# Five exponent buffers, another order at the handover, and other engines for the early block's split

## The chip, the cores and the metric

One NeuronCore of a Trainium2 chip runs the whole program. The metric is the device time of one execution in microseconds, the median of several runs.

## The reference, cut to what matters

The program is an attention with capped scores, followed by a mixture of experts in which every token goes to one expert of eight. All numbers are 32-bit floats.

```python
# q, k, v: 8 batches, 12 heads, 448 positions, 64 wide
scores = q @ k.T / sqrt(64)
scores = cap * tanh(scores / cap)
attn = exp(scores - max); attn /= attn.sum(-1) + 1e-9
x = (attn @ v) as 3584 tokens of 768
# w_gate 768x8, w1 8x768x1024, w2 8x1024x768
e = argmax(x @ w_gate); g = softmax(x @ w_gate)[e]
out = g * (max(x @ w1[e], 0) @ w2[e])
```

## The kernel before, in words

**Attention.** The work is 24 quads, each four heads of one batch, and a quad has seven tiles of 64 keys, so there are 168 tiles in 84 steps of two tiles. In step k the program issues, for tiles 2k and 2k+1, the score products on TensorE (`scores`, tile `sp`, two PSUM buffers) and the tanh on ScalarE (`tanh`, from `sp` into half of a buffer `pt`). Then come the exponential of the step before on ScalarE (`expo(k-1)`, in place in `pt`) and, on TensorE, the products with the values for tiles 2k-6 and 2k-5 (`pv`, `values`, accumulated in `po`). VectorE then adds up exponentials (`adds(k-2)`, tiles `acc` and `p4`). One `pt` buffer holds a step, so `tanh` of step k can only start when `values` and `adds` have read step k-4: four buffers. The two `po` banks hold one quad. The first value product of a new quad is therefore held back by a step (`held`), until VectorE has copied the old quad out (`outp`, tile `ot`).

Between the steps run the routing of finished batches (`sums`, `logits`, `rec_p` on TensorE; `rec_v`, `log_v`, `route_v`, `place_v`, `turn` on VectorE), written into a table by step with `at` and carried out with `do`. Each engine takes its instructions in the order in which they are written. [...]

**The early block.** While batches 4 to 8 are still in attention, 448 tokens of the first three batches are collected for the first expert block, called -2. From step 66 on, each of its six column blocks k is scaled (`scale_x`), transposed (`trans_x`, tile `xt`, two buffers) and split into a high part `xh` and the remainder `xl` (`split_x`, before: both on GpSimd). These six pieces come three steps apart.

**The handover.** After the last step the two `sp` buffers become four other PSUM banks (`ps_h`, `ps_z`). TensorE then computes the remaining value products, with the first products of block -2 in between: `up_mm(-2, 0)` is 18 matmuls over `xh`, `xl` and the weights' high and low parts. The rest of the mixture of experts follows, eight more blocks after block -2, with `up_mm`, `up_ev` and `down` in turn, weights and tokens gathered by indirect DMA from GpSimd's queue. `RING` is the space, in bytes of each SBUF partition, for the descriptors of GpSimd's DMAs.

Of the kernel before, what the change touches and what calls it, by code (L numbers as in the profile page):

```python
# [4 lines left out]
F32 = mybir.dt.float32  # L5
# [5 lines left out]
ALU = mybir.AluOpType  # L11
# [4 lines left out]
B, H, S, D = 8, 12, 448, 64  # L16
# [7 lines left out]
QB = S // 32  # L24


RING = 4096
QN = 11
QR = QB - QN

# [96 lines left out]
def attention_moe(tc, qT, kT, vL, capd, wgL, w1a, w1b, w2a, w2b, cst, cmk, out):  # L127
    nc = tc.nc
    V, A, G, PE = nc.vector, nc.scalar, nc.gpsimd, nc.tensor
# [10 lines left out]
    op = pools("op")  # L140
    pb = pools("pb")
# [13 lines left out]
    m = {"xp": xp}  # L155
# [89 lines left out]
    pts = {}  # L245
# [14 lines left out]

    def tanh(t):
        if t % 2 == 0:
            pts[t // 2] = pb.tile([128, 2, 2, S], F32, name="pt", bufs=4)
        scale = qsc if t < KT else 1.0
        A.activation(out=pts[t // 2][:, t % 2], in_=sps.pop(t)[:, :, 0:S], func=AF.Tanh, scale=scale)  # L265

# [4 lines left out]
    def expo(k):  # L271
        A.activation(out=pts[k], in_=pts[k], func=AF.Exp, scale=capt)  # L272
# [464 lines left out]
    def width(j):  # L737
        return LARGE if large(j) else SMALL

    def groups(j):  # L740

        return QB if large(j) else 8
# [53 lines left out]
    def chunk(pool, name, at=(0, 0)):  # L796
        return [
            pool.tile([128, DM + 8], F32R, name=name + i)[:, o : o + DM] for i, o in zip("hl", at)
        ]
# [4 lines left out]
    def high(i, f, e=A):  # L804
        w, r = ((w1s, w1r), (w2s, w2r))[i - 1]
        (e.copy if e is A else e.tensor_copy)(out=w[f][0], in_=r[f // 4][:, f % 4, :])
# [88 lines left out]
    xts = {}  # L895

    def trans_x(j, k, g=None):
# [2 lines left out]
        xt = xts[j, k] = m["xp"].tile([128, LARGE], F32, name="xt", bufs=XT)[:, 0:n]  # L900
        V.transpose(out=xt.rearrange("p (q j) -> p q j", j=32), in_=xg[:, g, 32 * k : 32 * k + 32])  # L901

    def split_x(j, k, e, eh=A, g=None):
        g = g or slice(0, groups(j))
        c = slice(32 * g.start, 32 * g.stop)
        xt = xts.pop((j, k))
        xh = m["xh"][:, k, c]
        (eh.copy if eh is A else eh.tensor_copy)(out=xh, in_=xt)  # L908
        e.tensor_tensor(out=m["xl"][:, k, c], in0=xt, in1=xh, op=ALU.subtract)
# [19 lines left out]
    def up_mm(j, f, r=None):  # L929
        r = r or slice(0, width(j))  # L930
        xh, xl = m["xh"], m["xl"]
        wh, wl = w1s[f]
        if (j, f) not in phs:
            phs[j, f] = m["ps_h"].tile([128, 512], F32, name="ph")[:, 0 : width(j)]
        ph = phs[j, f][:, r]
        i = 0
        for k in range(KC):
            c = slice(128 * k, 128 * k + 128)
            for w, x in ((wh, xh), (wh, xl), (wl, xh)):
                PE.matmul(ph, w[:, c], x[:, k, r], start=i == 0, stop=i == 3 * KC - 1)  # L940
                i += 1
# [101 lines left out]
    def at(step, when, f, *a):  # L1043
        tasks.setdefault((step, when), []).append((f, a))
# [37 lines left out]
    n_first = (KT * B_FIRST * NQ - 1) // 2 + 11  # L1082
# [11 lines left out]
    for i in range(QB):  # L1094
        at(n_first + 8 + i, "v", load_x, -2, range(i, i + 1))
    for k in range(KC):
        t = n_first + 24 + 3 * k
        at(t, "v", scale_x, -2, range(k, k + 1))
        at(t + 1, "v", trans_x, -2, k)
        at(t + 2, "v", split_x, -2, k, G, G)  # L1100
    w1s[0] = chunk(xp, "w10")
    at(n_first + 20, "v", split_w1, 0, G, G)

# [11 lines left out]
    def values(k):  # L1115
        nonlocal held
        last = None
        ready = held + [2 * k - 6, 2 * k - 5]
        held = [ready.pop()] if ready[-2] % KT == KT - 1 else []
        for t in ready:  # L1120
            pv(t)
            if t % KT == KT - 1:
                last = t // KT
        return last
# [29 lines left out]
    m["ps_h"] = pools("ps_h", bufs=2, space=PSUM, side="right", **tw)  # L1154
    m["ps_z"] = pools("ps_z", space=PSUM, side="right", **tw)
    expo(STEPS - 1)
    assert values(STEPS) is None
    up_mm(-2, 0)
    high(1, 2)
    low(1, 2, G)  # L1160
    adds(STEPS - 2)
# [289 lines left out]
```

## Time and profile before

| | us |
|---|---|
| median of 3 runs | 805.44 (804.15 to 806.04) |
| profiled execution | 804.61 |
| its span, first to last instruction | 802.7 |
| attention steps, ScalarE's first tanh to its last exponential | 6.7 to 304.2 |
| block -2 and the eight others | 306.9 to the end |

The page gives busy shares over the whole span: TensorE 97%, VectorE 69%, ScalarE 56%, GpSimd 51%. They are means over stages with different limits, so each stage is read by itself. PE is TensorE's matmuls, PEld its weight loads, DVE is VectorE, ACT is ScalarE, POOL is GpSimd. "Idle before" is the time for which an engine had nothing to do before an instruction, with the instruction that ended it.

### The profile page before, as it was taken

The numbers are of one execution on the slowest core, as the hardware profiler recorded it, in microseconds if no ns is written. First come the engines' busy times: TensorE is split into PE (matmuls) and PEld (weight loads), VectorE is DVE, ScalarE is ACT, GpSimd is POOL, SyncE is SP. The second block draws the span as 40 slices with busy tenths as digits, with TensorE's granted clock in tenths as the row PEclk, the third lists the DMA queues.
The fourth block names the chain that finished last, engine by engine and source line by source line (L and its number), as shares of the span: only waits on it lengthen the run. The fifth ranks groups of instructions, "written<-read, shape, count | busy, mean of one in ns | idle before, by whom it ended". The sixth has DMA issues, their size and how long they took to land.

```text
span 802.7 us, 15069 instructions
## 1 busy us (share of the span) xinstructions
PE 780.4 (97%) x5984; PEld 571.4 (71%) x5984; DVE 551.7 (69%) x908; ACT 449.4 (56%) x534; POOL 411.4 (51%) x400
## 2 busy tenths in 40 slices
PE   8999999999999989999999999999999999999995
PEld 3343434343434436899999999999999999999995
DVE  2788897998899997878549448358347357357730
ACT  7999999999998992343334324224224233234520
POOL 1001330318474465353785784884884884764742
PEclk9999999999999999999999999999999999999998
DMA  8325573488879602493441133542510252454211
GB/s 283 102 107 162 118 210 129 116 228 208 236 171 254 187 17 58 81 345 112 165 172 41 51 109 140 212 135 109 218 50 31 67 183 98 173 190 165 71 57 52
DMA packets 37102, 112.62 MB, mean 140 GB/s; under 512 B 8609, under 2 KB 15699, under 8 KB 34464
## 3 DMA queue, kind: packets, MB, share of 16 engines
q0 software_dynamic: 18528, 63.93, 25.5%
q1 hardware_dynamic: 18208, 47.43, 19.0%
q8 instruction: 49, 0.80, 0.4%
q10 hardware_dynamic: 288, 0.23, 0.1%
q14 instruction: 29, 0.24, 0.1%
HBM read 101.69 MB, written 22.85 MB: 155 GB/s over the span
## 4 chain that ended last, share of the span: by engine, by line
PE 81%; ACT 7%; DVE 6%; issue 2%; POOL 2%; DMA 1%; POOLq 0%; DVEq 0%; ACTq 0%
PE ph L940 29%; PE y L975 22%; PE po L322 10%; PE sp L255 10%; PE y L983 4%; ACT pt L265 4%; ACT pt L272 3%; PE ms L349 2%; DVE acc L277 2%; POOL xg L745 1%; PE po L975 1%; PE z L975 1%; PE ms L975 1%; DMA xg<-xd,xi 1%; DVE ot L329 1%
## 5 line engine op out<-in xcount | busy, mean ns | idle before, releaser
L952 ACT ACTIVATE hb<-ph 128x448 fp32r<-128x448 f32 (+1 forms) x69 | 35.0, 508 | 264.1 <-PE ph L940 263.4
L745 POOL DMA_INDIRECT xg<-xd,xi x114 | 139.7, 1225 | 36.4 <-issue 27.0
L953 DVE SCALAR_TENSOR_TENSOR hb<-ph,hb 128x448 fp32r<-128x448 f32 (+1 forms) x69 | 39.5, 572 | 168.7 <-ACT hb L952 168.7
L255 PE MATMUL sp<-qk 64*64 64x448 f32 x1344 | 147.5, 549 | 5.3 <-ACT pt L265 5.2
L272 ACT ACTIVATE pt<-pt,capt 128x1792 f32<-128x1792 f32 x84 | 152.4, 1816 | 0.0
L265 ACT ACTIVATE pt<-sp 128x896 f32<-128x896 f32 x161 | 140.0, 934 | 16.4 <-DVE acc L277 6.8
L322 PE MATMUL po<-pt,vr 64*64 64x448 f32 x1344 | 144.5, 541 | 4.4 <-DVE ot L329 4.4
L755 POOL DMA_INDIRECT out<-ys,xi x98 | 104.4, 1066 | 27.3 <-issue 27.3
L322 PEld LDWEIGHTS po<-pt,vr 64*64 64x64 f32 x1344 | 54.0, 134 | 79.2 <-issue 69.0
L255 PEld LDWEIGHTS sp<-qk 64*64 64x64 f32 x1344 | 43.9, 132 | 82.0 <-ACT pt L265 57.3
L277 DVE TENSOR_TENSOR acc<-acc,pt 128x1792 f32<-128x1792 f32 (+1 forms) x36 | 61.5, 1707 | 4.1 <-ACT pt L272 4.1
L485 POOL DMA_DIRECT2D xd<-w2r x12 | 8.4, 710 | 104.8 <-DVE mx L456 104.6
L940 PE MATMUL ph<-xh,qk 128*128 128x448 f32 (+2 forms) x228 | 60.5, 340 | 0.0
L277 DVE TENSOR_TENSOR acc<-pt 128x896 f32<-128x896 f32 (+1 forms) x36 | 51.4, 1428 | 11.0 <-ACT pt L272 10.7
L516 POOL DMA_INDIRECT ids<-tokg,slots x32 | 43.5, 1360 | 25.6 <-DVE slots L510 16.5
L908 ACT CAST xh<-xt 128x448 fp32r<-128x448 f32 (+2 forms) x54 | 25.8, 490 | 33.5 <-DVE xt L901 33.5
L745 POOL DMA_INDIRECT w1r<-in_w1b,widx x7 | 10.5, 1495 | 66.4 <-DVE w17l L811 66.4
L940 PEld LDWEIGHTS ph<-xh,qk 128*128 128x128 f32 x228 | 40.8, 188 | 3.4 <-issue 0.7
L940 PE MATMUL ph<-xl,qk 128*128 128x448 f32 (+2 forms) x114 | 38.6, 339 | 0.0
L329 DVE COPY ot<-po 128x448 f32<-128x448 f32 x48 | 27.5, 614 | 15.5 <-PE po L322 15.4
L901 DVE STREAM_TRANSPOSE xt<-xg 128x448 f32<-128x448 f32 (+2 forms) x60 | 32.4, 549 | 1.4
L890 DVE TENSOR_TENSOR xg<-xg,sc 128x448 f32<-128x448 f32 (+2 forms) x60 | 30.2, 551 | 0.3
(368 smaller groups left out, 1789.9 us busy)
## 6 DMA issues: line engine op xcount, KB each, us to landing
vr<-in_vL SPq DMA_DIRECT2D x24, 448.0 KB, 4.9
qk<-in_qT SPq DMA_DIRECT2D x23, 448.0 KB, 5.9
qk<-in_kT SPq DMA_DIRECT2D x22, 448.0 KB, 5.8
xd<-yt POOLq DMA_DIRECT2D x16, 346.5 KB, 6.3
xd<-w2r POOLq DMA_DIRECT2D x12, 346.5 KB
w1r<-in_w1a SPq DMA_DIRECT2D x8, 384.0 KB, 7.1
w1r<-in_w1b SPq DMA_DIRECT2D x8, 384.0 KB, 8.0
w2r<-in_w2b SPq DMA_DIRECT2D x8, 384.0 KB, 8.8
```

The source lines that it names most:

```text
L255: PE.matmul(sp[w, r, 0:S], kr[h, c, 64 * g : 64 * g + 64], qr[h, c, :], start=True, stop=True)
L265: A.activation(out=pts[t // 2][:, t % 2], in_=sps.pop(t)[:, :, 0:S], func=AF.Tanh, scale=scale)
L272: A.activation(out=pts[k], in_=pts[k], func=AF.Exp, scale=capt)
L277: V.tensor_tensor(out=o, in0=a, in1=b, op=ALU.add)
L322: PE.matmul(pvs[m][c][w, 0:S], vr[r, g, j, :], pt[r, j, :], start=g == 0, stop=g == KT - 1)
L329: V.tensor_copy(out=ot, in_=pvs[m][c][:, 0:S])
L516: i = G.indirect_dma_start(out=ids, out_offset=bass.IndirectOffsetOnAxis(ap=slots[0:p, c : c + 1].bitcast(U32), axis=0), in_=tokg[0:p, c, ...
L745: G.indirect_dma_start(out=dst, out_offset=None, in_=src, in_offset=bass.IndirectOffsetOnAxis(ap=idx.bitcast(U32), axis=0), bounds_check=b ...
L755: i = G.indirect_dma_start(out=dst, out_offset=bass.IndirectOffsetOnAxis(ap=idx.bitcast(U32), axis=0), in_=src, in_offset=None, bounds_che ...
L940: PE.matmul(ph, w[:, c], x[:, k, r], start=i == 0, stop=i == 3 * KC - 1)
L953: V.scalar_tensor_tensor(out=hl, in0=ph, scalar=0.0, in1=hh, op0=ALU.max, op1=ALU.subtract)
L975: PE.matmul(y[k][:, 0:LARGE], w[:, c], h, start=f == 0 and i == 0, stop=f == FC - 1 and i == 2)
```

## The change

- `pt` has five buffers and not four.
- `RING` is 2048 bytes and not 4096.
- Of the early block, the high part is copied by ScalarE, between the two tanhs and the exponential of a step, and the low part is computed by VectorE at the end of that step. This is one step later than GpSimd's turn was. The sixth piece is scaled and transposed one step earlier.
- At the handover `up_mm(-2, 0)` is written before `values(STEPS)` and not after it.

```diff
-RING = 4096
+RING = 2048
...
-            pts[t // 2] = pb.tile([128, 2, 2, S], F32, name="pt", bufs=4)
+            pts[t // 2] = pb.tile([128, 2, 2, S], F32, name="pt", bufs=5)
...
+    def high_x(j, k):
+        A.copy(out=m["xh"][:, k], in_=xts[j, k])
+
+    def low_x(j, k):
+        V.tensor_tensor(out=m["xl"][:, k], in0=xts.pop((j, k)), in1=m["xh"][:, k], op=ALU.subtract)
...
-        t = n_first + 24 + 3 * k
+        t = n_first + 24 + 3 * k - k // 5
         at(t, "v", scale_x, -2, range(k, k + 1))
         at(t + 1, "v", trans_x, -2, k)
-        at(t + 2, "v", split_x, -2, k, G, G)
+        at(t + 3, "act", high_x, -2, k)
+        at(t + 3, "v", low_x, -2, k)
...
-    assert values(STEPS) is None
     up_mm(-2, 0)
+    assert values(STEPS) is None
```

TensorE at the handover, before (`sp` are the last scores, `po` value products, `ph` the products of block -2):

```order
L255 MATMUL sp<-qk 64x448 x8
L322 MATMUL po<-pt,vr 64x448 x16
L940 MATMUL ph<-xh,w10h 128x448
L940 MATMUL ph<-xl,w10h 128x448
L940 MATMUL ph<-xh,w10l 128x448
```

and now, with the 18 matmuls into `ph` shortened to their first three and last one:

```order
L255 MATMUL sp<-qk 64x448 x8
L322 MATMUL po<-pt,vr 64x448 x4
L946 MATMUL ph<-xh,w10h 128x448
L946 MATMUL ph<-xl,w10h 128x448
L946 MATMUL ph<-xh,w10l 128x448
...
L946 MATMUL ph<-xh,w10l 128x448
L322 MATMUL po<-pt,vr 64x448 x28
L946 MATMUL ph<-xh,qk 128x448
```

Only the last tile of the old quad (4 rows of `po`; the trace counts each as two) stays ahead of the block's products. The seven tiles of the last quad follow them in one piece.

VectorE in the last step, before (`ot` is the copy of the old quad out of PSUM, `xt` the sixth transposed piece):

```order
L901 STREAM_TRANSPOSE xt<-xg 128x448
L329 COPY ot<-po 128x448 x2
L277 TENSOR_TENSOR acc<-pt 128x896
L503 TENSOR_TENSOR pos<-ms,base 128x32
L505 TENSOR_TENSOR base<-base,ms 128x8
L507 TENSOR_TENSOR pos<-pos,ob 128x32
L510 TENSOR_REDUCE slots<-pos 128x4
L277 TENSOR_TENSOR acc<-pt 128x896
```

and now:

```order
L329 COPY ot<-po 128x448 x2
L277 TENSOR_TENSOR acc<-pt 128x896
L503 TENSOR_TENSOR pos<-ms,base 128x32
L505 TENSOR_TENSOR base<-base,ms 128x8
L507 TENSOR_TENSOR pos<-pos,ob 128x32
L510 TENSOR_REDUCE slots<-pos 128x4
L907 TENSOR_TENSOR xl<-xt,xh 128x448
L277 TENSOR_TENSOR acc<-pt 128x896
```

The sixth low part now stands on VectorE behind the copies, one addition and four small instructions. Its transpose stands a step ahead of where it was.

ScalarE over the last three steps, now (`xh` the fifth and the sixth high part, which before were not on this engine):

```order
L265 ACTIVATE pt<-sp 128x896 x2
L904 CAST xh<-xt 128x448
L272 ACTIVATE pt<-pt,capt 128x1792
L265 ACTIVATE pt<-sp 128x896 x2
L471 ACTIVATE ex<-df 128x32
L272 ACTIVATE pt<-pt,capt 128x1792
L265 ACTIVATE pt<-sp 128x896 x2
L904 CAST xh<-xt 128x448
L272 ACTIVATE pt<-pt,capt 128x1792 x2
L806 CAST qk<-w1r_117 128x768
```

An exponential waits behind each of the six casts.

## Rows read from the trace of the kernel before

**Rows 1.** The page, first section: busy time, share, instructions of each engine.
```profile
PE 780.4 (97%) x5984; PEld 571.4 (71%) x5984; DVE 551.7 (69%) x908; ACT 449.4 (56%) x534; POOL 411.4 (51%) x400
```

**Rows 2.** Busy time by stretch: length, PE, PEld, DVE, ACT, POOL, TensorE's clock, DMA.
```profile
240.00:303.00 63.00, 57.26 (x684) 25.18 (x678) 61.44 (x90) 56.92 (x54) 31.37 (x24) 0.99 0.56 156
...
304.00:306.00 2.00, 2.00 (x16) 1.21 (x12) 1.97 (x4) 0.91 (x2) 1.06 (x2) 0.57 0.00 0
```

**Rows 3.** ScalarE's waits from 26 to 240 us: us in total, times, longest.
```profile
ACT pt L265 <- DVE acc L277: 4.1, 3, 1.4
ACT pt L265 <- PE po L322: 4.1, 9, 0.7
```

**Rows 4.** Timeline of ScalarE: start, us, instruction, idle before it.
```profile
102.96 1.73 ACT L265 ACTIVATE pt<-sp 128x896 f32<-128x896 f32 x2 [0.72 <-PE po L322]
...
141.67 1.73 ACT L265 ACTIVATE pt<-sp 128x896 f32<-128x896 f32 x2 [1.35 <-DVE acc L277]
```

**Rows 5.** The chain that ended last, in order of time: start, us, work.
```profile
120.50 1.79 PE sp L255 x16
...
128.30 1.50 PE sp L255 x16
129.81 1.50 PE po L322 x16
```

**Rows 6.** Timeline of TensorE, one wait for ScalarE.
```profile
149.34 1.79 PE L255 MATMUL sp<-qk 64*64 64x448 f32 x16 [0.69 <-ACT pt L265]
```

**Rows 7.** Groups by shape, whole span: the same split on ScalarE and VectorE.
```profile
L908 ACT CAST xh<-xt 128x448 fp32r<-128x448 f32 x30 | 16.5, 568 | 16.5 <-DVE xt L901 16.5
...
L909 DVE TENSOR_TENSOR xl<-xt,xh 128x448 fp32r<-128x448 f32 x30 | 17.9, 596 | 0.6
```

**Rows 8.** Groups of VectorE by shape, 240 to 303 us: count, busy us, mean ns.
```profile
L277 DVE TENSOR_TENSOR p<-acc 128x896 f32<-128x896 f32 x5 | 6.0, 1208 | 0.1
...
L890 DVE TENSOR_TENSOR xg<-xg,sc 128x448 f32<-128x448 f32 x6 | 4.9, 809 | 0.0
...
L269 DVE TENSOR_SCALAR qk<-qk,qsc 128x896 f32<-128x896 f32 x4 | 3.9, 980 | 0.0
...
L478 DVE TENSOR_SCALAR gt<-gt 128x4 f32<-128x4 f32 x2 | 1.1, 540 | 0.1
```

**Rows 9.** Three of these groups from 100 to 220 us.
```profile
L277 DVE TENSOR_TENSOR p<-acc 128x896 f32<-128x896 f32 x9 | 9.7, 1073 | 0.2
...
L269 DVE TENSOR_SCALAR qk<-qk,qsc 128x896 f32<-128x896 f32 x10 | 6.8, 680 | 0.0
...
L478 DVE TENSOR_SCALAR gt<-gt 128x4 f32<-128x4 f32 x3 | 0.5, 179 | 0.1
```

**Rows 10.** Tile xg, 380 to 440 us: duration in ns, least, median, most.
```profile
L890 DVE TENSOR_TENSOR xg<-xg,sc x6: 619/620/626, 421.0 to 423.7; 128x448 f32<-128x448 f32 x6
```

**Rows 11.** Timelines of VectorE and of GpSimd at the same time.
```profile
297.17 1.78 DVE L890 TENSOR_TENSOR xg<-xg,sc 128x448 f32<-128x448 f32 x1
...
296.65 1.82 POOL L811 TENSOR_TENSOR qk<-w1r,qk 128x768 fp32r<-128x768 f32 x1
```

**Rows 12.** Timelines at the handover: TensorE, then ScalarE, then VectorE.
```profile
298.48 0.93 PE L322 MATMUL po<-pt,vr 64*64 64x448 f32 x8
302.76 4.19 PE L322 MATMUL po<-pt,vr 64*64 64x448 f32 x24 [3.34 <-DVE ot L329]
...
310.73 3.24 PE L322 MATMUL po<-pt,vr 64*64 64x448 f32 x32
...
300.69 3.50 ACT L272 ACTIVATE pt<-pt,capt 128x1792 f32<-128x1792 f32 x2
...
302.12 1.12 DVE L329 COPY ot<-po 128x448 f32<-128x448 f32 x2
```

**Rows 13.** Timelines of GpSimd and VectorE: gathers for the second block.
```profile
366.34 1.02 POOL L745 DMA_INDIRECT xg<-xd,xi  x1 [0.30 <-issue]
...
370.43 0.20 DVE L881 TENSOR_TENSOR sc<-xg,idt 128x42 f32<-128x42 f32 x1 [0.33 <-DMA xg<-xd,xi]
```

More of the change, by code (lines that the diff above doesn't have):

```diff
@@ L1156, in attention_moe @@
     expo(STEPS - 1)
+    up_mm(-2, 0)
     assert values(STEPS) is None
-    up_mm(-2, 0)
     high(1, 2)
```

## The prediction

> **What bounds the kernel now.** I read the page first: TensorE is busy for 97% of the span [rows 1]. A time can therefore only fall where TensorE waits or runs below its pace, and I looked for those places stage by stage. After the handover there are next to none, so whatever is won before about 314 us should move the rest of the program forward as a whole. In attention, the stretch from 240 to 303 us is the odd one [rows 2]: VectorE is busy for 61.4 of 63 us there, while TensorE is idle for 5.7 and ScalarE for 6.1. VectorE sets the pace in it, because the early block's scaling and transposing comes on top of its additions. Earlier, from 26 to 240 us, TensorE and ScalarE are nearly balanced, and ScalarE's waits name a missing `pt` buffer: 4.1 us for VectorE's additions, 4.1 us for a held-back value product [rows 3].
>
> **Five buffers, 26 to 240 us.** A wait of ScalarE is only worth what TensorE loses by it. Two kinds repeat, in a pattern of two batches (about 74 us).
> The first is the wait of 0.72 us for a value product [rows 4]. In the steps that follow, ScalarE sets the pace: the two score products then take 1.79 us in the chain, against 1.50 when nothing holds them, and the value products take 1.50 [rows 5]. So a step is 3.29 us there and 3.0 at TensorE's own pace. Four such steps offer 4 x 0.29 = 1.2 us, so an earlier ScalarE passes its whole 0.7 us on. It occurs twice before 240 us: 1.4 us. The other short waits of that kind fall where TensorE is working off the sums and has no gap, and I count them as nothing.
> The second is the wait of 1.35 us for an addition [rows 4]. Some eight microseconds later TensorE stands still for 0.69 us and its next score product is stretched by 0.29 us [rows 6]: 0.98 us lost of 1.35. It occurs three times: 2.9 us.
> Sum: 4.3 us. The ends: three times the bare 0.69, or 2.1 us, and all of ScalarE's waits for a buffer, 4.1 + 4.1 = 8.2 us [rows 3].
>
> **The split, 240 to 303 us.** GpSimd loses six copies and six subtractions; ScalarE gains six copies of 0.57 us and VectorE six subtractions of 0.60 us, as in the same shapes of later blocks [rows 7].
> ScalarE: five copies lie before the last step, 5 x 0.57 = 2.8 us, beside 6.1 us of idle time, most of which the fifth buffer frees. They cost nothing as long as VectorE is the later one. If that cover goes, they cost 2.8 us. An exponential is queued behind each, and value products and additions wait for it. A copy would wait if its `xt` were late; that transpose is issued two steps ahead.
> VectorE: five subtractions before the last copies, 5 x 0.60 = +3.0 us. Against this stands something that the list of removed instructions hides: VectorE is slowed by GpSimd. The same instructions take longer from 240 to 303 us than from 100 to 220 us [rows 8, 9]: the fold 1.21 against 1.07 us (five: 0.7), the scaling of q 0.98 against 0.68 (four: 1.2), the small scalar operation 0.54 against 0.18 (two: 0.7); and the scaling of the gathered rows takes 0.81 against 0.62 us [rows 8, 10] (six: 1.1). That is 3.7 us. One row of it stays: 1.78 us for a scaling at 297.17, under the subtraction of a weight split on GpSimd that the change leaves where it is [rows 11], 1.16 us above the usual. So 2.6 us go and 3.0 come: VectorE is 0.4 us later at the last copies. Ends: 3.0 us later if the slowing only moves, 0.7 us earlier if the weight split's share goes as well.
> The Trainium skill ("SBUF — State Buffer", section "Who interferes with whom") says that a VectorE instruction with two SBUF inputs and a GpSimd one that reads SBUF exclude each other for the whole of the one that started first. The pair at 297 us agrees [rows 11]. It also speaks against the change: the new subtraction has two SBUF inputs, so the weight split's last subtraction on GpSimd can hold it up; the price of that is worked out below from those rows.
>
> **The handover.** Before [rows 12]: the last value product of the old quad ends at 298.48 + 0.93 = 299.4. TensorE then waits until VectorE has copied the old quad out (302.12). The next 24 matmuls take 4.19 us, though 16 take 1.50 [rows 5], so 24 should take 2.25: the clock is at 0.57 of full speed after the wait, its lower level of 1.2 GHz [rows 2]. Then 18 matmuls of the block until 310.73 (3.8 us), and 32 more until 313.97. The work is 2.25 + 3.8 + 3.0 = 9.05 us in 14.55: 5.5 us are lost.
> After: the block's 18 matmuls need a PSUM bank from the last tanhs, which end before the exponential at 300.69, so they start by 300.8. The first 16 need nothing late and end near 304.2. The last two need the sixth `xl`. VectorE: copies at 302.12 + 0.4 = 302.5 until 303.6, one addition (1.07, as the fold of the same size [rows 9]) until 304.7, four small instructions of 0.18 [rows 9] until 305.4, the subtraction until 306.0. So TensorE waits about 1.8 us, ends the block's products at 306.4 and then runs 56 matmuls of value products in 5.25 us, until 311.65. The exponentials have been ready since 304.2. Against 313.97 that is 2.3 us won. What is late next is that subtraction. At the old VectorE pace minus 0.7 us it would be 3.4 us won; at plus 3.0 us it would be -0.3.
>
> **Ring.** Halving `RING` costs nothing if GpSimd never fills it. Its gathers are issued 1.3 us apart, waiting for nothing but the issue [rows 13]. That is the work that hides it; the price without it is in the slower rival.
>
> **Sum.** 804.61 - 4.3 - 2.3 = 798.0 us, made against the profiled execution, which lies 0.8 us below the median of 805.44 and within the three runs. I leave that difference in the range.
>
> **Rivals.**
> A, the buffers bring nothing: TensorE's own work sets the pace before 240 us, and an earlier ScalarE only waits for scores instead. For it speaks that most of the short waits fall where TensorE has no gap. Against it stands the 0.69 us idle after each long wait [rows 6]. Time: 804.61 - 2.3 = 802.3.
> B, the sixth low part comes late: GpSimd's last weight subtraction starts first and holds VectorE as in [rows 11], less the usual time, 1.78 - 0.62 = 1.2 us; TensorE then waits 3.0 us, nearly the 3.34 that cost it the clock, and loses the 4.19 - 2.25 = 1.9 us again. The handover is then worth 2.3 - 3.1 = -0.8. Time: 804.61 - 4.3 + 0.8 = 801.1. For it speaks that this subtraction follows the last exponential closely.
> C, slower: the halved ring makes GpSimd wait for descriptor space. Place: the 14 gathers for the second block, the last of which VectorE already waits for by 0.33 us [rows 13]. Thirteen intervals stand behind one another, so half a microsecond more for each is 6.5 us and eats the whole gain; that is the point from which it decides. If the interval doubles, from 1.3 to 2.6 us, it is 17 us: 804.61 - 6.6 + 17 = 815. Against it: with the larger ring nothing but the issue ends the gap of 0.30 us there, so there is no sign of a queue that is nearly full.
> D, no change: the copies on ScalarE (2.8 us) and the subtractions on VectorE take back what the buffers and the order bring, and each engine simply waits elsewhere. Time: 804.6.
> E, more: all 8.2 us of ScalarE's waits come back, and the handover brings 3.4. Time: 793.0.
>
> **How the numbers follow.** Forecast, 798.0 with 795.5 to 800.5 around it: 0.55. A 0.13, B 0.12, E 0.07, D 0.06, C 0.07. A measurement of this kernel tells 0.2%, 1.6 us, from no change. Faster by more than that are the forecast, A, B and E: 0.87. Within it is D: 0.06. Slower is C: 0.07. The range of 8 in 10 runs from 793.5, just short of E, to 802.5, which takes in A and B; it leaves out C, D and the edge of E, 0.2 together.
>
> **What would show it.** Buffers: ScalarE's waits for `acc` and `po` before 240 us are gone, and TensorE's 0.69 us waits too; if ScalarE waits for `sp` instead by as much and the steps keep their times, A is right. Split: VectorE's groups [rows 8] fall to their times of earlier [rows 9], but for the one under the weight split. Handover: `ph` starts right behind the old quad, TensorE's remaining wait names the subtraction of `xl`, and the clock stays at full speed until the value products end; a clock of half again shows B. Ring: the interval of the gathers stays at 1.3 us; a longer one shows C. The prediction is wrong at its root if the time won at 314 us is given back later, that is, if TensorE waits in the blocks behind, where now it does not.

## The result, and the profile after

The changed kernel takes 797.66 us (median of five executions, 797.43 to 799.21) against 805.64 for the kernel before in the same series. The ratio is 0.9904, with a 95% interval from 0.9888 to 0.9920. A later series gave 798.92 against 806.18, a ratio of 0.9912 (0.9897 to 0.9926). So the change makes the kernel faster by 7 to 8 us, and 798.0 us was forecast. Whether the terms behind that number were right is the question of the rest of this document; two of them were not.

The profiled execution of the changed kernel took 799.21 us with a span of 797.1, against 804.61 and 802.7 before: 5.6 us of span, less than the medians differ. Where the missing part lies is told under "The clock" below.

**Page.** The busy line of the changed kernel, which answers to [rows 1]:

```profile
PE 779.4 (98%) x5984; PEld 581.2 (73%) x5984; DVE 550.3 (69%) x914; ACT 451.1 (57%) x540; POOL 401.7 (50%) x388
```

**Before 240 us.** ScalarE's waits from 26 to 240 us in the changed kernel (what waited, for whom; total, times, longest):

```profile
ACT pt L265 <- PE sp L255: 9.6, 12, 1.6
```

The waits for a buffer, 4.1 us for `acc` and 4.1 us for `po` [rows 3], are gone. ScalarE now waits for scores instead, and nearly as long in all: 9.6 us, against 4.1 + 4.1 for buffers before. That is what rival A announced, but it is no proof of it: a pacemaker that moves to TensorE leaves the same trace. The times between fixed points have to tell, and they follow below.

**240 to 303 us.** The windows of the changed kernel (length; busy time of TensorE, its weight loads, VectorE, ScalarE and GpSimd; TensorE's clock; DMA), answering to [rows 2], and VectorE's groups in the same stretch, answering to [rows 8]:

```profile
240.00:303.00 63.00, 59.42 (x683) 30.55 (x675) 61.78 (x101) 60.01 (x59) 14.88 (x13) 1.00 0.54 149
...
302.00:304.00 2.00, 1.55 (x14) 0.81 (x18) 2.00 (x3) 0.83 (x2) 1.09 (x1) 1.00 0.00 0
```

```profile
L277 DVE TENSOR_TENSOR p<-acc 128x896 f32<-128x896 f32 x5 | 5.3, 1064 | 0.1
L890 DVE TENSOR_TENSOR xg<-xg,sc 128x448 f32<-128x448 f32 x5 | 4.7, 936 | 0.0
L907 DVE TENSOR_TENSOR xl<-xt,xh 128x448 fp32r<-128x448 f32 x6 | 4.3, 708 | 0.0
L269 DVE TENSOR_SCALAR qk<-qk,qsc 128x896 f32<-128x896 f32 x4 | 2.7, 676 | 0.0
L478 DVE TENSOR_SCALAR gt<-gt 128x4 f32<-128x4 f32 x2 | 0.3, 171 | 0.1
```

VectorE is still busy for 61.8 of 63 us. The fold, the scaling of q and the small scalar operation are back at their times of earlier [rows 9], as the prediction wanted. The scaling of the gathered rows is not: 0.94 us on average, more than the 0.81 of before [rows 8]. One row makes it so, and it is shown under "What the split does".

**The handover.** TensorE, then VectorE, of the changed kernel (start, duration, instruction, in brackets the idle time before it and who ended it), answering to [rows 12]:

```profile
296.70 0.93 PE L322 MATMUL po<-pt,vr 64*64 64x448 f32 x8
297.63 0.44 PE L946 MATMUL ph<-xh,w10h 128*128 128x448 f32 x1
...
302.45 0.47 PE L946 MATMUL ph<-xl,w10h 128*128 128x448 f32 x1 [1.32 <-DVE xl L907]
...
303.04 5.49 PE L322 MATMUL po<-pt,vr 64*64 64x448 f32 x56
308.46 0.47 PE L946 MATMUL ph<-xh,qk 128*128 128x448 f32 x1
...
299.12 1.12 DVE L329 COPY ot<-po 128x448 f32<-128x448 f32 x2
...
301.78 0.61 DVE L907 TENSOR_TENSOR xl<-xt,xh 128x448 fp32r<-128x448 f32 x1
...
303.31 2.70 DVE L277 TENSOR_TENSOR acc<-acc,pt 128x896 f32<-128x896 f32 x1
```

The block's products start right behind the old quad, the one wait behind it, 1.32 us, names the subtraction of the sixth `xl`, and the clock stays at full speed (1.00 in the windows from 298 to 306 us). This is the picture that the prediction drew. Its last copies come at 299.12, though, and not at 302.5.

**A ruler.** TensorE's log_p products (line 430) come once for each batch and are a fixed point in every kernel. The stretches between them repeat to some hundredths of a microsecond from one execution to the next, but for one. The last point is the start of the early block's second chunk, behind the value products, and "handover" is the time from the seventh log_p point to it. All in us, from the starts of these products in the timelines; "left" is what remains of the span:

| kernel | first at | to 2nd | to 3rd | to 4th | to 5th | to 6th | to 7th | handover | left |
|---|---|---|---|---|---|---|---|---|---|
| before | 65.79 | 34.41 | 39.38 | 34.74 | 39.39 | 35.51 | 40.57 | 24.11 | 488.8 |
| changed | 65.69 | 33.57 | 38.55 | 34.58 | 39.62 | 34.68 | 41.47 | 20.30 | 488.6 |
| changed, second profile | 65.32 | 33.58 | 38.56 | 34.59 | 39.73 | 34.77 | 41.49 | 20.31 | 487.5 |
| e1 buffers alone | 65.28 | 33.57 | 38.57 | 34.59 | 39.72 | 35.31 | 40.58 | 24.53 | 487.6 |
| e2 order alone | 65.81 | 34.42 | 39.40 | 34.74 | 40.19 | 35.54 | 40.56 | 20.35 | 488.8 |
| e3 split alone | 65.61 | 34.42 | 39.39 | 34.75 | 40.02 | 34.99 | 40.44 | 21.55 | 490.0 |
| e4 ring alone | 66.20 | 34.42 | 39.39 | 34.75 | 40.17 | 35.54 | 40.57 | 25.68 | 486.8 |
| e6 without split | 65.50 | 33.57 | 38.54 | 34.58 | 39.71 | 35.30 | 40.56 | 20.33 | 490.8 |
| e7 sixth low first | 65.39 | 33.57 | 38.56 | 34.58 | 39.24 | 34.75 | 41.47 | 18.70 | 488.0 |
| e8 old order | 65.53 | 33.57 | 38.56 | 34.59 | 39.87 | 34.80 | 41.49 | 21.56 | 488.7 |
| e9 e7 + first block later | 65.23 | 33.57 | 38.55 | 33.96 | 38.50 | 34.64 | 41.30 | 18.72 | 488.0 |
| e10 e7 + first chunk's weights | 65.34 | 33.57 | 38.56 | 34.58 | 38.55 | 33.86 | 41.47 | 19.54 | 490.5 |
| e11 four buffers | 66.16 | 34.41 | 39.39 | 34.74 | 39.40 | 34.98 | 40.42 | 20.31 | 487.5 |
| e12 e9 without second chunk's weights | 65.46 | 33.57 | 38.54 | 33.96 | 39.79 | 34.76 | 39.92 | 18.71 | 489.9 |

Three things can be read off at once. The stretches to the 2nd and to the 3rd point fall by 0.84 and 0.83 us with five buffers, everywhere and only then. The handover falls from 24 to 20.4 us or less with the new order, whoever splits; with the old order it falls to 21.6 where ScalarE and VectorE split (e3, e8). And the stretch to the 7th is 0.7 to 0.9 us longer where five buffers and the split come together, as long as GpSimd splits the second chunk's weights in it (not in e12).

### The profile page after: what moved, and what is told of

It is laid out like the page before. It is cut to its first block, busy times and chain, and to the rows that moved or that the text cites. A ratio compares the mean times of both kernels' runs of the same rounds, so it can differ in the third digit from the quotient of the medians.

```text
span 797.1 us, 15048 instructions
## 1 busy us (share of the span) xinstructions
PE 779.4 (98%) x5984; PEld 581.2 (73%) x5984; DVE 550.3 (69%) x914; ACT 451.1 (57%) x540; POOL 401.7 (50%) x388
## 4 chain that ended last, share of the span: by engine, by line
PE 48%; issue 4%; POOL 3%; DVE 3%; DMA 1%; ACT 0%; POOLq 0%; DVEq 0%
PE ph L946 23%; PE y L981 20%; PE y L989 4%; DVE ys L1011 1%; POOL xg L745 1%; POOL out L755 1%; DMA xg<-xd,xi 1%; DVE xt L901 0%; DVE xl L915 0%; DMA out<-ys,xi 0%; DVE xg L890 0%; POOL ids L516 0%; POOL w2r L745 0%; POOL beat L1027 0%; DVE hb L959 0%
## 5 line engine op out<-in xcount | busy, mean ns | idle before, releaser
L272 ACT ACTIVATE pt<-pt,capt 128x1792 f32<-128x1792 f32 x84 | 154.9, 1846 | 0.0
L265 ACT ACTIVATE pt<-sp 128x896 f32<-128x896 f32 x161 | 142.5, 964 | 12.4 <-PE sp L255 12.4
L755 POOL DMA_INDIRECT out<-ys,xi x98 | 107.9, 1101 | 27.2 <-issue 26.7
L322 PEld LDWEIGHTS po<-pt,vr 64*64 64x64 f32 x1344 | 58.8, 133 | 71.2 <-issue 57.4
L255 PEld LDWEIGHTS sp<-qk 64*64 64x64 f32 x1344 | 49.3, 132 | 72.0 <-issue 32.8
L516 POOL DMA_INDIRECT ids<-tokg,slots x32 | 49.3, 1541 | 30.4 <-DVE slots L510 21.0
L485 POOL DMA_DIRECT2D xd<-yt x16 | 10.5, 658 | 64.8 <-DVE df L458 64.8
```

The lines of the kernel that those rows point to most:

```text
L255: PE.matmul(sp[w, r, 0:S], kr[h, c, 64 * g : 64 * g + 64], qr[h, c, :], start=True, stop=True)
L322: PE.matmul(pvs[m][c][w, 0:S], vr[r, g, j, :], pt[r, j, :], start=g == 0, stop=g == KT - 1)
L516: i = G.indirect_dma_start(out=ids, out_offset=bass.IndirectOffsetOnAxis(ap=slots[0:p, c : c + 1].bitcast(U32), axis=0), in_=tokg[0:p, c, ...
L755: i = G.indirect_dma_start(out=dst, out_offset=bass.IndirectOffsetOnAxis(ap=idx.bitcast(U32), axis=0), in_=src, in_offset=None, bounds_che ...
```

## The experiments

### The parts alone

**e1, five buffers alone**, with the halved ring.

```
-RING = 4096
+RING = 2048
...
-... name="pt", bufs=4)
+... name="pt", bufs=5)
```

> The kernel before with five buffers of exponents (and the halved ring), nothing else. Theory 1, the recorded sum: 4.3 us faster, TensorE's last log_p event at about 285.5 us instead of 289.8. Theory 2, read from the trace of after: the first long wait gives 1.7 us back, then VectorE, which has no idle time from about 137 us on, caps the rest; 1.7 to 2 us faster, the event near 288. Rival A: nothing, within 0.5 us.

Measured: ratio 0.9935 (0.9918 to 0.9952), 801.6 against 806.5 us. By the medians the gain is 4.9 us, which is theory 1's size. By the stretches, theory 2 is nearer: the seventh point is at 287.62 us, where theory 1 had 285.5 and theory 2 had 288. From the first to the seventh point it takes 222.34 us, against 224.0 in the profile of before and 224.8 in e2 and e4, so 1.7 to 2.5 us; with what is won before the first point it is 2.2 to 3.4. The rest of the 4.9 us does not lie before the seventh point. TensorE at the handover and two windows there:

```profile
300.60 4.28 PE L322 MATMUL po<-pt,vr 64*64 64x448 f32 x24 [3.36 <-DVE ot L329]
```

```profile
302.00:304.00 2.00, 2.00 (x16) 0.75 (x8) 1.97 (x4) 0.00 (x0) 2.00 (x1) 0.55 0.00 0
304.00:306.00 2.00, 2.00 (x8) 1.13 (x5) 1.97 (x4) 0.00 (x0) 1.21 (x2) 0.60 0.00 0
```

The wait of 3.36 us and the fall of the clock to its lower level stand there as before [rows 12]. How long the clock stays down differs between executions (see "The clock"), and part of the rest may be that. In the profiles 1.9 us of it are at the end of the program, which takes 7.6 us behind TensorE's last product here and 9.5 before. That end may go with the ring (see "The rest of the program").

**e2, the new order alone.**

```
-    assert values(STEPS) is None
     up_mm(-2, 0)
+    assert values(STEPS) is None
```

> The kernel before with the early block's products put ahead of the value products at the handover, nothing else. In the kernel before the sixth low part is ready at about 304.05 us, when 16 of the 18 block products can just have ended, so TensorE should not wait for it. The value products then end near 309.5 to 310 us instead of 313.9. Theory 1 and theory 2 both: about 4 us faster, the clock at full speed from 300 to 304 us. If the clock falls all the same after a short wait: 2 us faster.

Measured: ratio 0.9943 (0.9931 to 0.9956), 801.7 against 806.5 us: 4.8 us, close to what both theories said. Its timeline of TensorE:

```profile
304.98 0.47 PE L940 MATMUL ph<-xl,w10h 128*128 128x448 f32 x1 [0.45 <-POOL xl L909]
...
305.58 5.49 PE L322 MATMUL po<-pt,vr 64*64 64x448 f32 x56
311.01 0.47 PE L940 MATMUL ph<-xh,qk 128*128 128x448 f32 x1
```

There is a wait of 0.45 us for GpSimd's low part, where none was expected, instead of 1.32 for VectorE's; before the first block product TensorE waits 0.78 us for a tanh. The granted clock is 1.00 in all windows from 298 to 306 us. The handover takes 20.35 us, as much as in the changed kernel. In these profiles the order alone brings the whole of the handover's gain.

**e3, the split alone.**

```
-        t = n_first + 24 + 3 * k
+        t = n_first + 24 + 3 * k - k // 5
...
-        at(t + 2, "v", split_x, -2, k, G, G)
+        at(t + 3, "act", high_x, -2, k)
+        at(t + 3, "v", low_x, -2, k)
```

> The kernel before with the early block's high parts on ScalarE and its low parts on VectorE, one step earlier for the last, nothing else. Theory 1, the recorded step: VectorE's last copies of the old quad come 0.4 us later, so 0.4 us slower, within 0.2% of before. Theory 2, from the trace of after: VectorE is relieved by more than it takes on, since GpSimd's weight split moves to an earlier place too; the last copies come 1.4 us earlier, and TensorE's wait of 3.34 us falls to about 2; 1.4 us faster, and up to 3.3 us if the clock then stays up.

Measured: ratio 0.9987 (0.9972 to 1.0001), 804.78 against 806.5 us. That is not told from no change. VectorE and TensorE in its timelines:

```profile
292.62 0.58 DVE L890 TENSOR_TENSOR xg<-xg,sc 128x448 f32<-128x448 f32 x1
...
300.56 1.13 DVE L329 COPY ot<-po 128x448 f32<-128x448 f32 x2
...
301.21 3.00 PE L322 MATMUL po<-pt,vr 64*64 64x448 f32 x24 [1.71 <-DVE ot L329]
```

The last copies stand 10.94 us behind the seventh point (300.56 - 289.62), against 12.33 before (302.12 - 289.79, [rows 12] and the table): 1.39 us earlier, where +0.4 was forecast. The scaling that took 1.78 us under GpSimd's weight split [rows 11] takes 0.58, because that split is no longer there. Two small instructions that the prediction did not count are released too: lines 440 and 446, 0.56 and 0.57 us before, take 0.19 and 0.25 here. In this profile the clock stayed at full speed after a wait of 1.71 us. Half of the kernel's twelve executions report a mean clock of 0.994, the others 0.996 or 0.997, so in these it probably fell.

**e4, the ring alone.**

```
-RING = 4096
+RING = 2048
```

> The kernel before with the halved descriptor ring, nothing else. Theories 1 and 2: no change, within 0.5 us, with the gathers still issued 1.3 us apart. Rival C: the interval grows, and the time by thirteen times the growth.

Measured: ratio 0.9984 (0.9972 to 0.9995), 805.35 against 806.5 us: 1.15 us less, a difference below the 0.2% that can be told from none, though the interval leaves out 1. The stretches up to the seventh point are those of e2. GpSimd's gathers for the second block, against [rows 13]:

```profile
367.68 1.00 POOL L745 DMA_INDIRECT xg<-xd,xi  x1 [0.30 <-issue]
368.99 1.08 POOL L745 DMA_INDIRECT xg<-xd,xi  x1 [0.30 <-issue]
```

The interval is still 1.3 us with the same 0.30 us of issue. Rival C is out. The end of the program is shorter here than before, though, and that is taken up below.

### The changed kernel, with one part undone

**e5, the changed kernel again.** It has no edit.

> The changed kernel again, for a second profile beside the following runs. All theories: 797.5 us, with TensorE's remaining wait of about 1.3 us at the handover for VectorE's subtraction of the sixth low part, and the clock at full speed from 300 to 304 us. If the first profile was a slow execution in attention, the last log_p event of this one comes before 288.2 us.

Measured: 798.92 us, ratio 0.9912 (0.9897 to 0.9926). The stretches are those of the first profile, and so is the wait, 1.33 us. The last log_p event comes at 288.04 us, against 288.16 in the first profile, so that one was no odd execution in attention; what differs between the two is the rest of the span (488.6 and 487.5 us).

**e6, without the split**: the kernel before with the edits of e1 and e2.

> The changed kernel with the split given back to GpSimd: five buffers, the new order, the halved ring. Theory 1, the recorded step: VectorE comes 0.4 us later with the split, so this kernel is 0.4 us faster or as fast as the changed one, and TensorE's wait for the sixth low part is shorter. Theory 2, read from the parts run alone: the split makes VectorE 1.4 us earlier at the last copies, but with the new order nobody waits for these copies, so the kernels are equal within 0.5 us; TensorE's wait names GpSimd and is 0.5 to 1.1 us.

Measured: 798.57 us, ratio 0.9897 (0.9878 to 0.9915), not to be told from the changed kernel in the same series. TensorE:

```profile
302.06 0.47 PE L940 MATMUL ph<-xl,w10h 128*128 128x448 f32 x1 [0.76 <-POOL xl L909]
```

Theory 2 holds: with the new order nobody waits for the last copies, so VectorE's 1.4 us are worth nothing there. The split moves the wait for the sixth low part from GpSimd (0.21 + 0.76 us) to VectorE (1.32), and the handover stays at 20.3 us.

**e8, with the old order**: the changed kernel with the edit of e2 undone.

> The changed kernel with the old order at the handover. Theory 1: the handover as before but VectorE's copies 0.4 us later, so the whole 2.3 us and a little more are lost: 800.5 us. Theory 2: the copies come 1.4 us earlier by the split, TensorE's wait is 1.7 to 2.4 us instead of 3.3, and the clock falls in some executions only; 799 to 801 us, with the executions apart by up to 2 us.

Measured: 800.04 us (799.87 to 800.81), ratio 0.9921 (0.9908 to 0.9935): 1.1 us more than the changed kernel's 798.92. TensorE:

```profile
300.01 3.00 PE L322 MATMUL po<-pt,vr 64*64 64x448 f32 x24 [2.13 <-DVE ot L329]
```

The time does not part the theories (800.5, and 799 to 801). The wait does: 2.13 us, as theory 2 had it. After it the clock stayed at full speed in this profile, and the mean clock of all five executions, 0.997 or 0.998, gives no sign of a fall; here the expected spread of 2 us did not come. So the split and the order are two ways to the same thing: each shortens the wait of 3.34 us, and the handover falls to 21.6 or 20.3 us. Together they bring no more there than the order alone.

**e11, with four buffers**: the changed kernel with the edit to `bufs` undone.

> The changed kernel with four buffers. Theory 1, the recorded sum: 4.3 us slower than the changed kernel, 802.3 us. Theory 2, from the stretches between the log_p events: 224 to 224.9 us from the first to the seventh event instead of 222.5, so 1.5 to 2.4 us slower, 799.5 to 800.5, with the handover unchanged at 20.3 us and no fall of the clock.

Measured: 799.09 us (798.98 to 799.49), ratio 0.9922 (0.9909 to 0.9936), against 0.9904 and 0.9912 for the changed kernel. By the ruler the seventh point comes 1.3 to 1.5 us later (289.50 against 288.16 and 288.04); 0.6 to 0.9 of it lie between the first and the seventh point, 223.34 us where 224 to 224.9 were expected. Theory 1, 4.3 us, falls. Theory 2 has the direction and the handover, 20.31 us; its 1.5 to 2.4 us are too much. In the company of the split the fifth buffer is worth about 1.4 us.

### Where the buffers' gain stops

In the first pair of batches (first to third point) five buffers give 0.84 + 0.83 = 1.67 us. The prediction had 0.7 + 0.98 = 1.68 for a pair and let the pattern repeat. The pieces agree less well than the sum: 0.84 for the forecast 0.98, and 0.83 for 0.7. In the second pair (third to fifth point) they give 0.16 and then nothing that stands out. The third long wait lies in the stretch to the sixth point, where they give 0.2 (35.51 to 35.31 in e1); e10, below, takes another 0.89 off that stretch by moving GpSimd's split of the first weight chunk. The same place in the two pairs, in the changed kernel: VectorE and TensorE at the quad's sums, first pair, then second pair.

```profile
82.95 1.09 DVE L277 TENSOR_TENSOR p<-acc 128x896 f32<-128x896 f32 x1
...
84.70 1.41 PE L349 MATMUL ms<-p,cs 128*32 128x352 f32 x24
...
153.05 0.12 DVE L534 TENSOR_TENSOR cnt<-base,kc 128x8 f32<-128x8 f32 x1
...
154.58 0.15 DVE L544 CAST t0i<-t 128x1 int32<-128x1 f32 x1
154.66 2.02 DVE L277 TENSOR_TENSOR acc<-acc,pt 128x1792 f32<-128x1792 f32 x1
156.71 1.09 DVE L277 TENSOR_TENSOR p<-acc 128x896 f32<-128x896 f32 x1
...
156.83 0.79 PE L349 MATMUL ms<-p,cs 128*32 128x352 f32 x4
157.85 1.40 PE L349 MATMUL ms<-p,cs 128*32 128x352 f32 x20 [0.24 <-DVE p L277]
```

Counted from the point before, the fold starts at 82.95 - 65.69 = 17.26 us in the first pair and at 156.71 - 137.81 = 18.90 in the second: 1.6 us later. What stands ahead of it only there are nine small instructions of the first block (lines 534 to 544, 153.05 to 154.66 us). TensorE begins the sums and has to stop after four of 24 products: from their first to the score product behind them it is 2.35 us (156.83 to 159.18), instead of 1.35.

**e9, the first block's small instructions two steps later**, on top of e7 (below):

```
-    at(n_first, "v", first_block)
-    at(n_first + 1, "v", first_rows)
-    at(n_first + 2, "v", first_row)
+    at(n_first + 2, "v", first_block)
+    at(n_first + 3, "v", first_rows)
+    at(n_first + 3, "v", first_row)
```

> The changed kernel with the sixth low part first (as in the run before) and, new, the first block's small instructions on VectorE two steps later. Theory: in the second pair of batches the fifth buffer gives less, because ten small instructions (1.6 us) stand ahead of an addition and the fold, the fold ends 1.6 us later than in the first pair, and TensorE's sums wait for it; moved behind it, the stretch between the log_p events at 137.5 and 172.1 falls from 34.58 us to 33.57, as in the first pair, and the kernel is 1 us faster than the run before: 796.3 us. Rival: TensorE or ScalarE set the pace there and the stretch keeps its 34.6 us.

Measured: 794.73 us (794.58 to 794.96), ratio 0.9868 (0.9853 to 0.9883). VectorE and TensorE in its timelines:

```profile
154.61 1.09 DVE L277 TENSOR_TENSOR p<-acc 128x896 f32<-128x896 f32 x1
...
157.43 0.15 DVE L534 TENSOR_TENSOR cnt<-base,kc 128x8 f32<-128x8 f32 x1
...
156.37 1.41 PE L349 MATMUL ms<-p,cs 128*32 128x352 f32 x24
```

The fold is back at 17.26 us behind the point (154.61 - 137.35), and the sums run through. The stretch to the fourth point falls from 34.58 to 33.96 us, not to 33.57: 0.62 of the 1.0 us. The other 0.4 us lie at the point itself, for which TensorE waits 0.22 us on VectorE's `lr` (171.31; the product before it starts 0.66 us earlier, and 0.28 in the first pair). The rival, that TensorE or ScalarE set the pace there, falls; VectorE caps the stretch to the fourth point. Most of the rest of e9's gain over e7 lies in the stretch to the fifth point (38.50 against 39.24), and that is not shown to come from the edit: e12, with the same edit, has 39.79 there, and e10, without it, 38.55.

### What the split does

The split's copies and subtractions left GpSimd, and so the second chunk's weight split, which stood behind ten of them in GpSimd's queue and had its subtraction at 296.65 us [rows 11], now has it at 270.73. GpSimd and VectorE in the changed kernel:

```profile
269.55 1.09 POOL L806 CAST qk<-w1r 128x768 fp32r<-128x768 f32 x1
270.73 2.08 POOL L811 TENSOR_TENSOR qk<-w1r,qk 128x768 fp32r<-128x768 f32 x1
...
269.88 1.25 DVE L907 TENSOR_TENSOR xl<-xt,xh 128x448 fp32r<-128x448 f32 x1
271.05 2.25 DVE L890 TENSOR_TENSOR xg<-xg,sc 128x448 f32<-128x448 f32 x1
273.21 1.14 DVE L329 COPY ot<-po 128x448 f32<-128x448 f32 x2
```

A scaling of 0.62 us [rows 10] takes 2.25, and the new subtraction 1.25 instead of 0.61 (the one at 301.78). Each ends 0.5 us behind the end of the GpSimd instruction beside it (270.64 and 272.81). The copies that TensorE's value products wait for come behind these two. With four buffers the same pair takes 0.62 and 1.25 us (e3, 272.36 and 272.90), and the stretch is no longer than before.

One stretch earlier the split is a gain: the stretch to the sixth point falls by 0.5 to 0.6 us with it (35.54 to 34.99 from e2 to e3, 35.30 to 34.68 from e6 to the changed kernel). Which of the removed GpSimd instructions does it was not tried.

**e10, the weights of a chunk split on ScalarE and VectorE**, on top of e7:

```
-    at(n_first + 20, "v", split_w1, 0, G, G)
+    at(n_first + 37, "v", split_w1, 0, V, A)
```

> The changed kernel with the sixth low part first and, new, the weight split that stands on GpSimd under VectorE's subtraction and scaling at 269 to 273 us done by ScalarE (0.83 us) and VectorE (0.95 us) instead. Theory: the split's cost with five buffers, 41.47 us against 40.56 from the sixth to the seventh log_p event, is this collision (1.24 and 2.25 us for instructions of 0.57 and 0.62); without it the stretch falls to 40.5 to 40.9 us, while VectorE is 0.95 us later for the weights themselves, so 0.5 to 1 us faster than 797.3. Rival: ScalarE's six high parts cost the 0.9 us; then the stretch stays at 41.5 or grows by 0.8.

Measured: 798.14 us, ratio 0.9910 (0.9895 to 0.9926), no better than e7. The experiment did not do what its text says: the edit moves the split of the first chunk, and the one at 269 to 273 us is that of the second. So the stretch to the seventh point stays at 41.47, and decides nothing between the theories. By accident it tests the same thing in another place: the first chunk's split stood on GpSimd at 221 to 225 us, and without it the stretch to the sixth point falls from 34.75 to 33.86 us. VectorE's 0.92 us for the weights then stand at 286.48, ahead of `ob`, for which TensorE waits 1.21 us instead of 0.34, and the handover is 0.84 us longer. The gain is given back.

**e12, no split of the second chunk**, on top of e9. It leaves work out:

```
-            split_w1(1, G, G)
...
-        wh, wl = w1s[f]
+        wh, wl = w1s[0 if j < 0 and f == 1 else f]
```

> The run with the first block later and the sixth low part first, without GpSimd's split of the second weight chunk in attention (left out: the early block's second chunk is multiplied with the first chunk's weights, so the output is another). Theory: the 0.9 us that the split of the block costs with five buffers between the sixth and the seventh log_p event is this weight split at 267 to 271 us, which holds VectorE's subtraction (1.24 us) and scaling (2.25 us); without it both take 0.6 us, and the stretch falls from 41.30 us to 40.2 to 40.6. Rival: ScalarE's high parts, 0.57 us each, set it; then the stretch stays at 41.2 or more.

Measured: the stretch to the seventh point falls from 41.30 us in e9 to 39.92, more than expected. VectorE's two instructions there:

```profile
269.27 0.62 DVE L907 TENSOR_TENSOR xl<-xt,xh 128x448 fp32r<-128x448 f32 x1
269.80 0.62 DVE L890 TENSOR_TENSOR xg<-xg,sc 128x448 f32<-128x448 f32 x1
```

TensorE's wait of 0.79 us for `ot`, which e9 has at 271.47, is gone. So the 0.9 us that the split costs with five buffers is GpSimd's weight split at its new place, not ScalarE's six high parts; these are still there in e12. The kernel's time, 797.21 us (ratio 0.9888, 0.9871 to 0.9904), is not that of e9 less 1.4: the stretch to the fifth point was 39.79 in its profile, and the rest of the span 489.9.

### The last wait

**e7, the sixth low part ahead of the old quad's copies**:

```
-        at(t + 3, "v", low_x, -2, k)
+        at(t + 3, "act" if k == KC - 1 else "v", low_x, -2, k)
```

> The changed kernel with the sixth low part put ahead of the old quad's copies on VectorE. Theory: TensorE's last wait of 1.3 us is on that subtraction and on nothing else, so it goes, and the copies, later by one subtraction of 0.6 us, are still ready before the 16 block products end. 1.2 us faster than the changed kernel (796.3 us). Rival: the block's products wait for something else that is as late, or the additions behind come late and take it back; then no change.

Measured: 797.26 us against 798.92 for the changed kernel in the same series, ratio 0.9891 (0.9874 to 0.9908). TensorE:

```profile
300.83 5.49 PE L322 MATMUL po<-pt,vr 64*64 64x448 f32 x56
306.26 0.47 PE L946 MATMUL ph<-xh,qk 128*128 128x448 f32 x1
```

The handover falls from 20.31 to 18.70 us, 1.6 us, and TensorE no longer waits behind the old quad. The subtraction was the only thing that it waited for there. With this and the first block moved, e9 is the fastest kernel of the study, 10.7 us below the kernel before in its series (805.44).

## Why the prediction was right, step by step

The time was right, and that is in part luck: the sum was made of one term too large and one too small. In the two profiles the 5.6 us of span are 1.63 up to the seventh point (forecast: 4.3 by the buffers), 3.81 in the handover (forecast: 2.3), 1.95 lost from there to TensorE's last product, and 2.11 won after it (forecast: nothing in either place).

- **The bound.** Right for the stretch to the seventh point. There VectorE sets the pace: 2.3 us taken off it in e12 are 1.4 us off the stretch.
- **Five buffers, 4.3 us.** Too large. The step that failed is "it occurs three times". The first occurrence was well sized (1.68 worked out, 1.67 measured), but the pattern of two batches is one of ScalarE and TensorE alone; in the second pair VectorE has other work ahead of the fold, and at the third occurrence the gain is 0.2 us. By the seventh point the fifth buffer is worth 2.2 to 3.4 us when alone (287.62 against 289.79, 290.66 and 291.04 in the profiles of before, e2 and e4), and about 1.4 us in the changed kernel (e11), which is below the lower end of 2.1. The medians of e1 alone, 4.9 us, would not have told it from 4.3.
- **The split, VectorE 0.4 us later.** Wrong in sign at the last copies: 1.4 us earlier (e3), twice the end of 0.7 that it gave for this case. The step that failed is "under the subtraction of a weight split on GpSimd that the change leaves where it is". The program leaves it; the queue does not. With ten instructions gone from ahead of it, GpSimd came to it 26 us earlier. The price went with it, and was paid there: 1.25 and 2.25 us instead of 0.6 each, 0.9 us of TensorE's time (the stretch to the seventh point). The rest of the 1.4 us, about 0.7, is the size of what lines 440 and 446 give back. For the whole the split is worth nothing that can be measured (e6): 0.6 us won before the sixth point, 0.9 lost before the seventh.
- **The Trainium skill against the change** ("SBUF — State Buffer", section "Who interferes with whom"): a VectorE instruction with two SBUF inputs and a GpSimd one that reads SBUF exclude each other. The rows of 269 to 273 us agree (2.25 us against 0.62), and e12, with GpSimd's instructions left out, shows that these were the cause. The rule was right that a new subtraction would be held, but it was an earlier one of the six. The sixth was over at 302.39, before GpSimd's last weight subtraction began at 302.91; that one met the addition behind it (2.70 us, 303.31), for which TensorE does not wait. So rival B did not come.
- **The handover, 2.3 us.** Too small: 24.11 to 20.30 us, 3.8 us in the profiled executions. The direction and the mechanism were right, and the wait of about 1.8 us was 1.32. The term that was mis-sized is VectorE's, by the step that failed under the split: the sixth `xl` was put at 306.0 us, and is ready at 302.39; with the 1.63 us by which the seventh point comes earlier, that is 304.0 on the clock of before, 2 us earlier than worked out; the copies account for 1.75 of it (299.12 + 1.63 against 302.5). The block's products also start earlier, at 299.3 on that clock and not at 300.8: with five buffers nothing holds them, with four they wait 0.78 and 0.96 us for a tanh (e2, e11).
- **Ring and rivals.** The ring costs nothing, as said, so C is out; that it might win something was not considered. A's sign is in ScalarE's waits, but the stretches are shorter. D and E would have put the time at 804.6 and 793.0 us.
- **The rest of the program.** Not quite rigid. The sign that the prediction named, TensorE waiting in the blocks behind, is there. In the first profile of the changed kernel TensorE waits twice for VectorE's `hb`, in the second once for 0.32 us, and in the profile of before not at all. Two waits and the start of the last product, changed kernel:

```profile
376.52 0.47 PE L981 MATMUL y<-hb,w20h 128*128 128x448 f32 x1 [0.57 <-DVE hb L959]
...
495.01 0.47 PE L981 MATMUL y<-hb,w20h 128*128 128x448 f32 x1 [0.62 <-DVE hb L959]
...
789.74 0.33 PE L989 MATMUL y<-w27h,hb 128*128 128x384 f32 x1
```

and the last product before:

```profile
793.23 0.33 PE L983 MATMUL y<-w27h,hb 128*128 128x384 f32 x1
```

From the end of the handover to TensorE's last product it is 479.33 us before (793.23 - 313.90), and 481.28 and 480.15 in the two profiles of the changed kernel: 0.8 to 1.9 us are given back. That is small against the gain, so the root of the prediction holds, but it is not nothing. The column "left" hides this, because the end of the program takes 9.5 us behind the last product in the profile of before and 7.4 in both of the changed kernel. It is the last transfer to `out` that lands sooner: 4.7 us after GpSimd has issued it, against 6.8. Over all profiles this end goes with the ring. It takes 9.3 to 9.5 us in the three kernels with 4096 bytes (before, e2, e3) and 7.3 to 7.7 in nine of the eleven profiles with 2048, but 9.7 and 9.9 in the other two (e12, e10). So up to 2 us of the gain, and of that of e1, may be the ring's, which the forecast put at nothing. It is not shown: no run changes the ring in the finished kernel, and the two exceptions say that the ring is not all.

**The clock.** The two medians differ by 8.0 us and the profiled executions by 5.4. Of the missing 2.6 us, 1.0 lies on the side of before (804.61 in the profile, 805.64 in the median) and 1.6 on the other: the profiled execution of the changed kernel, 799.21 us, is the slowest of five. That part is not the clock's, since all five report a mean clock of 0.997 or 0.998; it stays open.

Before, TensorE's clock falls to its lower level, 1.2 GHz, after the wait of 3.34 us [rows 12], and is back at full speed (1.00) from 306 us in the profiled execution. So it is in e1, which has two windows below full speed, 0.55 and 0.60. In e4, which has the same wait at the same place, the clock is at the lower level for 6 us at least:

```profile
304.02 5.28 PE L322 MATMUL po<-pt,vr 64*64 64x448 f32 x24 [3.35 <-DVE ot L329]
```

```profile
304.00:306.00 2.00, 1.98 (x10) 1.24 (x14) 2.00 (x2) 2.00 (x2) 1.22 (x2) 0.50 0.22 62
306.00:308.00 2.00, 2.00 (x16) 1.13 (x10) 1.97 (x4) 0.16 (x1) 1.76 (x1) 0.50 0.00 0
308.00:310.00 2.00, 2.00 (x10) 0.73 (x3) 1.97 (x4) 0.00 (x0) 1.21 (x2) 0.50 0.00 0
```

The handover is 25.68 us there and 24.11 in the profile of before. Each execution reports its mean granted clock, and over 50 executions of the kernel before that number orders the spans: 0.993 in 18 of them (median span 805.2 us), 0.995 in 17 (803.9), 0.997 in two (802.1 and 802.2). The eleven executions of the changed kernel all report 0.997 or more. So the kernel before seems to lose 2 to 3 us to the clock in most executions, and the changed kernel does not. Where the clock fell is seen in profiles alone; the mean takes in the whole span, and the changed kernel's profile has 0.94 from 780 to 795 us, where TensorE runs out of work. The prediction counted the 1.9 us of one profile.

**Still open.** The stretch to the fifth point takes 38.5 to 40.2 us, by execution and not by edit as far as these runs go. In e12 a score product at 184.93 us takes 2.10 us there, where the one of e9 takes 1.80, and ScalarE then waits 0.63 us for it. What held it was not tried. Nor was it tried what makes VectorE late with `hb` behind the handover, and what sets the 2 us at the end of the program, the ring or something else.

## What to carry to other kernels

When instructions leave an in-order queue, look at what stands behind them in that queue: it moves up, and takes its collisions with it. When a pattern of waits repeats, check each repetition against every engine before multiplying, since the second one may have other work in its way. And parts that shorten the same wait do not add up: alone, the split and the order took 2.6 and 3.8 us off the handover here, together 3.8 (e3, e2, e11); undo each from the finished change to see what it is worth. Last, a time that comes out as forecast does not prove its terms: look for the signs that were named, where the time was to be given back too.

## What the runs showed of the hardware

The same wait of TensorE, 3.34 to 3.36 us at one place of one program, was followed by two windows of 2 us below full speed in two profiles (0.58 and 0.57, 0.55 and 0.60) and by three at 0.50 in another, and the times of the kernel before, 803.9 to 809.2 us, follow the mean clock. Waits of 1.32, 1.71 and 2.13 us there were followed by full speed in the profiles, though half of the executions with the wait of 1.71 us report a lower mean clock.

An instruction of VectorE on 128 x 32 numbers, 0.18 us by itself (e7, 301.39 us), can take 1.5 us beside GpSimd: the one of line 507 took 1.52 us there while GpSimd split the first chunk's weights.

```profile
222.36 2.56 POOL L811 TENSOR_TENSOR w10l<-w1r,w10h 128x768 fp32r<-128x768 f32 x1
...
223.44 1.52 DVE L507 TENSOR_TENSOR pos<-pos,ob 128x32 f32<-128x32 f32 x1
```
